# Even weight rows of the second mixer, loaded in two halves of the contraction

## The chip, the cores and the metric

The kernel runs on one core of one Trainium2 chip. The metric is the device time of one execution in microseconds (us), as a median of several runs. A profile is one further execution, recorded instruction by instruction.

## The reference

The input `x` has 2048 tokens of width 1024. A linear-attention block and a mixer over tokens follow each other, each behind a layer norm and with a residual. All inputs are bfloat16.

```python
h  = x + A(layernorm(x), wqkv, wo)      # linear attention, 32 heads
h2 = h + B(layernorm(h), w1, b1, w2, b2)

def B(x, w1, b1, w2, b2):               # S = 2048 tokens, F = 3584
    h = layernorm(x)
    u = gelu(einsum("bsd,sf->bdf", h, w1) + b1)
    y = einsum("bdf,fs->bds", u, w2) + b2
    return transpose(y)
```

The change lies in the last product, `u @ w2`: a contraction over F = 3584, with 2048 output tokens. In the text this is the second mixer; `u @ w1`'s counterpart before it is the first.

## The kernel before

**Seven products.** Each large product is made by a Strassen-like scheme of seven products instead of eight. For one pair index `p` (256 output tokens) the weights form four blocks: rows of `w2` are taken in tiles of 128, even tiles and odd tiles of the contraction, and each has two column halves of 128. The blocks `a11` and `a21` come from the even rows (`even[p % 2]`), `a12` and `a22` from the odd rows (`odd[p]`). One set of even or odd rows is a tile of 128 partitions x 14 x 256 bfloat16, 896 KB, read from HBM in runs of 512 bytes. Sums and differences of blocks (`asum`) are made by DVE. The difference for product 7 is written over `a21`, so the even rows are in use until product 7 has read them.

**Quads.** The second mixer has eight values of `p`, taken in pairs: quad `u` holds `p = 2u` and `2u + 1`. Quad 0 is the prologue, quads 1 to 3 run through `Quad.run2`. In a quad, products 1, 5, 2 and 3 of its two matrices are themselves made by a second level of seven smaller products (`Inner`, with steps `i1` to `i7`). Products 6, 7 and 4 are not; their matmuls are cut into pieces and put between the steps of the inner levels as filling (`interleave`). The last half of a quad's product 4 fills the next quad's first inner level.

**Two buffers of even rows.** There are two buffers of even rows, so the even rows of the next quad go where those of this quad lie. They can be loaded only when product 7 of the matrix in question is done. In quads 1 to 3, product 7 runs in four parts of seven matmuls each (`pieces`): the first half of the contraction for both matrices, then the second half for both. In the prologue product 7 runs whole, for one matrix and then the other.

**Order on the queues.** Most operations of this part are pinned to the order in which the program states them. All its loads go through the queue of SP (`hd`), which works in order: an issue that waits holds up those behind it. Around the change, SP has: the reload of a parked operand for product 4 (`load("p7")`, `reload(4, 0)`), which waits until both matrices' first half of product 7 has read the buffer `gs0`; the even rows of the next quad (`next2`, `load_w2(p, 0, hd)`); then, at the end of `run2`, the reload of the parked operand for product 7 (`load("in3")`), and in the next quad the odd rows (`load("in1")`). Outputs are added to HBM by accumulating stores from POOL's queue (line 487).

**Who reads the new even rows.** `begin_next` (called between the steps `i7` and `i4` of the quad's last inner level, at "third") makes the next quad's first two inner sums on DVE: the first reads the second matrix' `a11`, the next one adds the first matrix' `a11`. Step `i1` of the next quad's first inner level reads the first matrix' `a11` directly, step `i6` reads the two sums.

Line 230 is that of a helper (`Held`) that pins an operation, so most rows of this part carry L230; tiles tell them apart. `wq` is a weight tile that holds even rows, odd rows and two output buffers; `w2o` are odd rows of two further buffers; `gs` the derived moving operands for products 7 and 4; `is` the inner sums; `psI` the inner products' accumulators; `psC` that of products 7 and 4.

Of the kernel before, what the change touches and what calls it, by code (L numbers as in the profile page):

```python
# [10 lines left out]
P = 128  # L11
# [19 lines left out]
def kernel(  # L31
# [12 lines left out]
    nc = tc.nc  # L44
# [85 lines left out]
    NFP, NSP = NF // 2, NS // 2  # L130
# [20 lines left out]
    even, odd, ots = {}, {}, []  # L151
# [2 lines left out]
    def w2_view(t):  # L154
        return t.rearrange("p (k f) -> p k f", f=2 * P)

    def load_w2(p, second, q=nc.sync):
        q.dma_start(
            (odd[p] if second else even[p % 2]),
            B_w2[:, p * 2 * P:(p + 1) * 2 * P].rearrange("(k two p) s -> p k two s", two=2, p=P)[:, :, second, :],  # L160
        )

    def first_w2(p):
        t = w_tile(wpool, WLEN)
        ots.extend(t[:, 2 * WH + o:2 * WH + o + CW] for o in (0, CW))
        even[p], odd[p] = w2_view(t[:, 0:WH]), w2_view(t[:, WH:2 * WH])
        odd[p + 4] = odd[p]
        for second in (0, 1):
            load_w2(p, second)
# [63 lines left out]
    hv, ht, hs, hd = (Held(e, True) for e in (nc.vector, nc.tensor, nc.scalar, nc.sync))  # L233
# [1462 lines left out]
    spans = (slice(0, H2), slice(H2, NFP))  # L1696
# [46 lines left out]
    for p in (2, 3):  # L1743
        odd[p] = odd[p + 4] = w2b.tile([P, NFP, 2 * P], BF16, tag=f"o{p}", name=f"w2o{p}")[:]
        load_w2(p, 1)
# [5 lines left out]
    def quad2(u):  # L1751
        return Quad([Mixer2(2 * u), Mixer2(2 * u + 1)], mov1, mov5, mov2, mov3)
# [5 lines left out]
    def next2(u):  # L1758
        if u == NSP // 2:
            return None  # L1760
        for p in (2 * u, 2 * u + 1):
            load_w2(p, 0, hd)
        return quad2(u)

    def loads(u):
# [35 lines left out]
    for st in pend:  # L1801
        st.p7()
    nxt = next2(1)
    run_all(make_t4)
    pend[1].p2()
# [11 lines left out]
    for u in range(1, NSP // 2):  # L1817
        rest, nxt = nxt.run2(
            rest, lambda: next2(u + 1), loads(u), first if u == 1 else (nop,) * 4, CW - P if 2 * u + 2 == NSP else None,
        )  # L1820
# [34 lines left out]
```

## Time and profile before

| what | value |
|---|---|
| median of 3 runs | 557.47 us (557.39 to 557.54) |
| the profiled execution's own time | 559.21 us |
| its span, first to last instruction | 557.4 us |
| mean granted TensorE clock | 0.997 |
| TensorE matmul busy | 549.4 us, 99% of the span |
| DVE, ACT, POOL busy | 444.8, 289.1, 26.3 us |
| loads of even and odd rows into `wq` | 12 of 896 KB, 7.9 us to landing in the median |
| DMA over the whole span | 74.58 MB, 134 GB/s |

The page names the engines PE (TensorE matmul), PEld (its weight loads), DVE (VectorE), ACT (ScalarE), POOL (GpSimd) and SP (SyncE, which here only issues DMAs). A row of the timeline gives start, length, engine, line, operation and the tiles out<-in; in brackets stands how long the engine had been idle before it, and what released it. A row of the table of stages gives for a stretch of time the busy time of each engine, then the granted clock of TensorE, the busy share of the 16 DMA engines and their GB/s.

The second mixer begins at about 390 us; its quads 1, 2 and 3 begin at 425, 468 and 511 us.

### The profile page before, as it was taken

Reading aid. Unit: us, or ns where it says so; the run is one execution under the profiler, and the core shown is the slowest. Engines: PE = TensorE matmul, PEld = TensorE weight load, DVE = VectorE, ACT = ScalarE, POOL = GpSimd, SP = SyncE. Lnnn points to the kernel's source line nnn. Section 1 sums busy time; section 2 is a strip of 40 time slices with the busy share of each in tenths; the row PEclk is TensorE's granted clock in tenths of the full one; section 3 lists DMA queues with packets and bytes.
Section 4 is the critical chain, followed back from the end, with each engine's and each line's share of the span. In section 5 each row is a group of like instructions: output and inputs, shape, how many; then the busy total and the mean of one; then the engine's idle time right before and its main releaser. Section 6 shows DMA issues by size and latency. Waiting matters only on the chain.

```text
span 557.4 us, 9806 instructions
## 1 busy us (share of the span) xinstructions
PE 549.4 (99%) x3819; PEld 315.6 (57%) x3819; DVE 444.8 (80%) x863; ACT 289.1 (52%) x614; POOL 26.3 (5%) x36
## 2 busy tenths in 40 slices
PE   8999999999999999999999999999999998999997
PEld 3444446644444444456666666766445665667665
DVE  7798888755597798879988989788986878649747
ACT  5747778766877777635556546464112312413311
POOL 1000000000000000000000000000002102103111
PEclk9999999999999999999999999999999999999999
DMA  8933341205668932104043140440957948749433
GB/s 295 310 77 76 86 87 20 39 1 176 202 183 257 304 148 76 56 1 153 0 152 100 53 152 11 141 113 22 284 187 179 258 133 205 175 132 235 93 108 74
DMA packets 82991, 74.58 MB, mean 134 GB/s; under 512 B 15730, under 2 KB 74368, under 8 KB 82944
## 3 DMA queue, kind: packets, MB, share of 16 engines
q1 hardware_dynamic: 78560, 69.87, 42.1%
q0 software_dynamic: 4096, 3.68, 4.8%
q8 instruction: 30, 0.49, 0.4%
q10 hardware_dynamic: 288, 0.39, 0.2%
q14 instruction: 17, 0.14, 0.1%
HBM read 59.12 MB, written 11.67 MB: 127 GB/s over the span
## 4 chain that ended last, share of the span: by engine, by line
PE 94%; DMA 4%; SPq 1%; DVE 0%; ACT 0%; issue 0%; DVEq 0%
PE psI L230 24%; PE acc_t L230 15%; PE psC L230 15%; PE psB L230 8%; PE psC L973 4%; PE psB L973 4%; PE psA L973 4%; PE acc_t L893 3%; PE acc_t L1302 2%; PE psA L342 2%; PE psB L342 2%; DMA wq<-in_B_w_dram 2%; PE psE L973 2%; PE psC L342 2%; DMA wkv<-in_A_wqkv_dram 1%; PE psA L230 1%
## 5 line engine op out<-in xcount | busy, mean ns | idle before, releaser
L230 PEld LDWEIGHTS <-is 128*128 128x128 f16 x736 | 71.8, 98 | 33.7 <-DVE is L230 2.5
L230 PEld LDWEIGHTS <-sa 128*128 128x128 f16 x606 | 59.2, 98 | 27.2
L230 PEld LDWEIGHTS <-wq 128*128 128x128 bf16 (+1 forms) x496 | 48.8, 98 | 28.6 <-issue 1.0
L230 PE MATMUL acc_t<-wo_sb,pqT 128*128 128x512 f16 x256 | 55.6, 379 | 0.0
L487 POOL DMA_DIRECT2D out_dram<-wq x28 | 24.4, 935 | 519.1 <-DVE sa L334 396.3
L230 PEld LDWEIGHTS <-pqT 128*128 128x128 bf16 x256 | 24.9, 98 | 30.5 <-issue 0.6
L230 DVE TENSOR_TENSOR t<-psI,t 128x256 f32<-128x256 f32 (+1 forms) x45 | 20.8, 476 | 22.2 <-PE psI L230 20.9
L230 PE MATMUL psC<-gs,wq 128*128 128x512 f16 x140 | 34.1, 380 | 0.0
L973 PEld LDWEIGHTS <-xs 128*128 128x128 f16 x208 | 19.7, 98 | 22.3 <-DVE xs L962 0.8
L190 DVE TENSOR_SCALAR e_sb<-e_sb 128x512 bf16<-128x512 bf16 x64 | 18.4, 288 | 17.1 <-ACT e_sb L185 16.8
L230 PE MATMUL psC<-hT,sa 128*128 128x512 f16 x112 | 31.2, 380 | 0.0
L230 PE MATMUL psI<-hi,is 128*128 128x256 f16 x200 | 30.0, 273 | 0.0
L230 PE MATMUL psB<-hT,sa 128*128 128x512 f16 x112 | 29.7, 380 | 0.0
L230 PE MATMUL acc_t<-xnT,wq_sb 128*128 128x512 bf16 x128 | 29.0, 380 | 0.0
L230 DVE BATCH_NORM_STATS2 hst<-acc_t 128x6 f32<-128x512 f32 x32 | 21.4, 692 | 8.9 <-ACT h_bf L230 8.9
L185 ACT ACTIVATE e_sb<-acc_t 128x512 bf16<-128x512 f32 x32 | 19.1, 597 | 17.3 <-PE acc_t L1302 9.5
L973 PE MATMUL psA<-wkv,xnT 128*128 128x512 bf16 x104 | 26.7, 379 | 0.0
L973 PEld LDWEIGHTS <-xnT 128*128 128x128 bf16 x156 | 15.2, 98 | 18.7 <-issue 1.1
L230 DVE TENSOR_TENSOR e<-psI,es 128x256 f32<-128x256 f32 x20 | 8.5, 425 | 20.8 <-PE psI L230 20.8
L230 ACT CAST h_bf<-acc_t 128x512 bf16<-128x512 f32 x32 | 18.4, 584 | 12.4 <-PE acc_t L230 12.0
L230 PE MATMUL psI<-gi,is 128*128 128x256 f16 x168 | 22.7, 276 | 2.0 <-DVE is L230 2.0
L230 PE MATMUL psC<-hT,wq 128*128 128x512 f16 x96 | 24.6, 379 | 0.0
(245 smaller groups left out, 1117.3 us busy)
## 6 DMA issues: line engine op xcount, KB each, us to landing
wq<-in_B_w_dram SPq DMA_DIRECT2D x14, 1024.0 KB, 7.8
wq<-in_B_w_dram SPq DMA_DIRECT2D x12, 896.0 KB, 7.9
gs<-parked SPq DMA_DIRECT2D x9, 896.0 KB, 4.9
shared_sb<-rd_dram SPq DMA_DIRECT2D x32, 128.0 KB, 4.2
out_dram<-h_bf SPq DMA_DIRECT2D x16, 256.0 KB, 2.0
x_sb<-in_A_x_dram SPq DMA_DIRECT2D x14, 256.0 KB, 3.0
w2o<-in_B_w_dram SPq DMA_DIRECT2D x4, 896.0 KB, 10.2
out_dram<-wq POOLq DMA_DIRECT2D x28, 128.0 KB, 5.1
```

The source lines that it names most:

```text
L185: pin(nc.scalar.activation(e_sb[:], src, ACT.Exp))
L190: pin(nc.vector.tensor_scalar(e_sb[:], e_sb[:], 1.0, PHI_EPS, ALU.min, ALU.add))
L230: return (lambda *a, **kw: pin(op(*a, **kw))) if self.always or getattr(Held, self.key) else op
L342: pe.matmul(ps[:, cols], lhsT=lhs[:, k, :], rhs=mv(k)[:, cols], start=(start and k == 0), stop=(k == self.nk - 1), skip_group_check=True,)
L487: nc.gpsimd.dma_start(to, ot[:, a:b], accum_op=ALU.add)
L893: mm = nc.tensor.matmul(pp[:, 0:CW], lhsT=xnT[:, kt, i * P:(i + 1) * P], rhs=wkv[:, kt, c * CW:(c + 1) * CW], start=(kt == 0), stop=(kt == ...
L973: pin(nc.tensor.matmul(ps[:], lhsT=lhs[:, k, :], rhs=rhs[:, k, :], start=(start and k == 0), stop=(k == hk2 - 1), skip_group_check=True,))
L1302: nc.tensor.matmul(qp[:, 0:SW], lhsT=wq_sb[:, kt, j * P:(j + 1) * P], rhs=xnT[:, kt, u * SW:(u + 1) * SW], start=(kt == 0), stop=(kt == ND ...
```

## The change

`load_w2` gets a range of the contraction, `ks`, which is all 14 tiles unless given. `next2` loads the even rows of the next quad's two matrices in two halves of 7 tiles: first the first half of both matrices, then the second half of both. A load of 896 KB becomes two of 448 KB; runs remain 512 bytes. As the first halves overwrite only the first seven tiles of each buffer, they have to wait only for the first half of product 7. Nothing else is moved. `spans` is `(slice(0, 7), slice(7, 14))`, which was there before.

```diff
-    def load_w2(p, second, q=nc.sync):
+    def load_w2(p, second, q=nc.sync, ks=slice(0, NFP)):
         q.dma_start(
-            (odd[p] if second else even[p % 2]),
-            B_w2[:, p * 2 * P:(p + 1) * 2 * P].rearrange("(k two p) s -> p k two s", two=2, p=P)[:, :, second, :],
+            (odd[p] if second else even[p % 2])[:, ks, :],
+            B_w2[:, p * 2 * P:(p + 1) * 2 * P].rearrange("(k two p) s -> p k two s", two=2, p=P)[:, ks, second, :],
         )
...
     def next2(u):
         if u == NSP // 2:
             return None
-        for p in (2 * u, 2 * u + 1):
-            load_w2(p, 0, hd)
+        for ks in spans:
+            for p in (2 * u, 2 * u + 1):
+                load_w2(p, 0, hd, ks)
         return quad2(u)
```

`next2` is called three times, for quads 1, 2 and 3.

## The prediction

> **What bounds the kernel now.** First the page: one engine fills the span, so only an idle or slow stretch of TensorE can be worth anything.
>
> ```profile
> PE 549.4 (99%) x3819; PEld 315.6 (57%) x3819; DVE 444.8 (80%) x863; ACT 289.1 (52%) x614; POOL 26.3 (5%) x36
> ```
>
> The list of waits for 400 to 557 us, where the second mixer runs, then says where TensorE stops and what stands behind it. Columns: who waited for whom, total us, times, longest.
>
> ```profile
> DVE is L255 <- DMA wq<-in_B_w_dram: 4.2, 1, 4.2
> ...
> DVE is L230 <- DMA wq<-in_B_w_dram: 2.5, 1, 2.5
> ...
> PE psI L230 <- DVE is L230: 2.0, 1, 2.0
> ```
>
> DVE waits twice for the even rows that the change touches. Only one of these waits reaches TensorE, once, for 2.0 us. The timeline shows that place, the start of quad 2 (first column: start in us; second: length; in brackets: idle before and its releaser).
>
> ```profile
> 453.53 0.34 SPq L230 DMA_DIRECT2D gs<-parked  x1
> ...
> 456.57 2.64 SPq L230 DMA_DIRECT2D wq<-in_B_w_dram  x2
> ...
> 467.79 0.93 PE L230 MATMUL psI<-gE,wq 128*128 128x256 f16 x7
> ...
> 470.25 0.63 DVE L230 TENSOR_TENSOR is<-wq 128x896 f16<-128x896 bf16 x1 [2.54 <-DMA wq<-in_B_w_dram]
> ...
> 471.60 1.38 PE L230 MATMUL psI<-gi,is 128*128 128x256 f16 x7 [2.02 <-DVE is L230]
> ...
> 475.67 0.93 PE L230 MATMUL psI<-gE,is 128*128 128x256 f16 x7
> ```
>
> The table of stages, cut to 1 us, adds the clock (the column after POOL is PEclk, then the DMA share and GB/s).
>
> ```profile
> 457.00:458.00 1.00, 1.00 (x7) 0.51 (x6) 0.66 (x2) 0.20 (x1) 0.00 (x0) 1.00 0.46 146
> 458.00:459.00 1.00, 1.00 (x8) 0.60 (x7) 0.97 (x2) 0.52 (x1) 0.18 (x1) 1.00 0.99 268
> ...
> 470.00:471.00 1.00, 0.00 (x0) 0.00 (x0) 0.71 (x2) 0.00 (x0) 0.00 (x0) 1.00 1.02 316
> ...
> 473.00:474.00 1.00, 1.00 (x6) 0.72 (x5) 1.00 (x2) 0.36 (x1) 0.83 (x1) 0.50 0.00 0
> ```
>
> The idle is followed by half clock. The clock record puts it at 471.94 to 475.35, the only such stretch between 4.3 us and the end.
>
> **The price of that stall.** From the start of i1 (467.79) to the start of i5 (475.67) quad 2 takes 7.88 us. The same instructions of quad 3 run from 511.18 to 515.20, 4.02 us, without idle and at full clock. So the stall costs 3.86 us. TensorE's work before i6 would have let it start at 469.41 and it started at 471.60, which is 2.19; the other 1.67 are the slow clock.
>
> **Why the load is late.** A DMA adds one to its completion count for each of the 16 DMA engines. Quad 2 holds the matrices p4 and p5 (pair indices 4 and 5). The counts say that the load for p4 (issued 456.57) was done on 15 engines at 462.00 and on the last at 464.55. The load for p5 (issued 458.84) was done at 466.94 and 470.23. One DMA engine was 3.29 us behind. The sums take 1.37 us from landing to i6 (470.23 to 471.60), so the last landing that costs nothing is 469.41 - 1.37 = 468.04; it came 2.19 too late. In quad 3 the loads had landed by 510.02 and DVE reached its sums only at 511.02; that quad gains nothing. In quad 1 DVE waits 4.17 us and has its sums at 424.93, i6 starts at 427.94, with no idle before it: it gains nothing either and stands 3.0 us of lateness.
>
> **The change, part by part.**
>
> Removed and moved: two loads of 896 KB become four of 448 KB, three times. In quads 2 and 3 the queue of SP is in order: the reload for product 4 (t4, 453.53) stays ahead, because it waits for the first half of the seventh products of both matrices, and that is also what both first halves wait for. They follow at once, at about 453.9 and 454.3 (one issue takes 0.37). The second halves wait for what the whole loads waited for: 456.57 and 458.84. So half of the bytes are issued 2.7 and 4.5 us earlier.
>
> How much earlier does the last byte land? The DMA engines had no work left only for a while: share 0.46 in 457 to 458 and 0.99 or about that from there on. So 0.54 us of transfer can move ahead; with the ramp of 455 to 456 (share 0.75) 0.79. Rows of 512 bytes went at 482 per us before the stores came (2894 packets from 458 to 464), which is 33 ns each on an engine, so 16 to 24 packets of each engine move. At the end they stand in turn with the accumulating stores of 1024 bytes (101 ns a packet, from 463.9). By the packets that were left, 15 engines end near 465.5 instead of 466.94. If the last engine keeps its lag it ends near 469.2, 1.0 earlier; if its lag is 2.5 us or less, as it was for p4, it ends by 468.05 and the stall is gone. So the idle left lies between 0 and 1.2 us; I take 0.5. An idle of 0.54 us at 6.2 us in this trace was not followed by a slow clock, and 2.02 was; so I count no slow clock. Gain in the profiled execution: 3.86 - 0.5 = 3.36. Ends: 0.8 (0.8 us less idle, the slow clock stays) and 3.86.
>
> The Trainium skill, "TensorE: Matmul & The Clock Gate", Part 1, says that the clock halves after at least one idle window of about 3.4 us. By it 2.0 us of idle would cost no slow clock, and the whole stall 2.19 instead of 3.86; this trace shows 3.41 us of half clock behind 2.02 of idle, so the measurement decides.
>
> Added: two more issues on SP per quad, 0.37 us each. What SP has next in quad 2 is the reload at 467.21, 8 us after; nothing is late. The fixed part of two more transfers: at the first mixer two loads were issued 0.44 us apart (255.99, 256.43) and landed 5.2 and 8.0 us after issue, so a queued load takes 3.2 us more and not another 5.2. The fixed part lies beside the load ahead, and I count nothing; not covered, it would be 5.2 - 3.2 = 2.0 us, which would use up the advance.
>
> The page "DMA: Bandwidth & Descriptors", section "Measured (HBM→SBUF, 128 partitions, SWDGE, issued from GpSimd)", speaks against the change: it wants transfers of 1 MiB or more, and its fit of 2.0 us and the bytes makes a load of 448 KB 3.1 us, so four in a row 12.2 where two of 896 KB take 8.2, an estimate of 4 us lost. No run here shows halves of this load alone.
>
> More waits: DVE's first sum reads p5 whole, the second p4, TensorE's i1 p4; each now waits for two transfers. The first of each pair has landed by then, so nothing is added; the bound from the trace is one gap of an issue, 0.02 us in the chain of waits, to six times that.
>
> In quad 1 the seventh products of the two matrices run one behind the other (410.29 to 416.34). SP would issue the first halves for matrices 2 and 3 at about 411.8 and 414.9, then the second half for 2 at 415.2 instead of 413.35, that for 3 at 416.4 as now. The last landing stays within about 1 us of 423.63, under the 3.0 to spare. What is next late: with the stall gone nothing, by quad 3.
>
> **From the trace to the time.** The profiled execution took 559.21 us, of which the span is 557.44 and 1.77 lie around it. The median of the runs is 557.47, 1.74 below. The trace doesn't say what these 1.74 are; they may be a shorter stall. So the gain in a timed run lies between 3.36 - 1.74 = 1.62 and 3.36, middle 2.5: 557.47 - 2.5 = 555.0. Its own range runs from the full 3.86 (553.6) to the least that can be told, 1.1 (556.4): the measurement tells about 0.2%, 1.1 us, from no change.
>
> **The rivals.**
>
> Same, 0.33: the late DMA engine belongs to this one execution. No other load behind 190 us has a lag over 1.2 us between the 15th and 16th engine. With a lag of 1.1 us p5's load would land at 468.04, exactly in time; then timed runs have no stall to lose, and the time stays at 557.2 to 557.6. Against it: the three runs agree within 0.15 us, and 1.74 is less than 3.86. The same result comes if the halves are not kept apart and the first ones wait for the whole seventh products: landing as before, 557.5. Against that: at 413.35 a part of tile wq is loaded while TensorE still has to read its other part (416.17).
>
> Slower, 0.17: the reload of the operand of product 4 (t4) no longer has the DMA engines to itself. It landed at 458.38 and its first reader ran at 460.18, 1.80 to spare (501.86 and 503.57 in quad 3, 1.71). Alone it takes 4.9 us; rows of the same transfer with a load 0.4 us behind it show 5.0 (479.45) and 6.0 (436.06), both inside that. Beyond 1.8 us it decides: with the lag of 3.29 on it, it lands at 457.90 + 3.29 = 461.19, TensorE stops for 1.0 and may lose 1.67 in clock. Where the old stall doesn't exist in timed runs, that is 557.47 + 1.0 to 2.7, 558.5 to 560.2.
>
> **How the numbers follow.** Faster 0.50 at 555.0 (553.6 to 556.4), same 0.33, slower 0.17. From 553.5 to 558.4 leaves out nearly all of the slower case, and a little below.
>
> **What would show it.** Right: four issues per quad, two right behind the reload near 454; the load's last landing before 468.04; no 2 us gap before i6, no half clock at 472; i1 to i5 of quad 2 near 4.0 us. Wrong: the first halves issued near 456.6; an equal landing; a gap before the first psC behind the reload of t4; or a stall-free quad 2 with an unchanged time, which would put the stall down to the one execution.

## The result, and the profile after

| | kernel before | changed kernel |
|---|---|---|
| median of 6 runs, us | 557.43 (557.12 to 557.72) | 555.52 (555.29 to 556.6) |
| ratio to the kernel before | | 0.9968, interval 0.9956 to 0.9981 |
| profiled execution's own time, us | 559.21 | 556.6 |
| its span, us | 557.4 | 554.8 |

By the medians the changed kernel is faster by 1.91 us, 0.34%. The ratios here and below are not those of the medians; they differ from them by up to 0.0013. The forecast was 555.0, in a range of 553.5 to 558.4.

The chain of waits on the page of the changed kernel has no DMA left in it (before, 4% of it was):

```profile
PE 98%; issue 0%; ACT 0%; DVE 0%; DVEq 0%
```

The list of waits for 400 to 557 us keeps one of the three rows shown before, that of quad 1. DVE still waits there, a little longer, and TensorE does not:

```profile
DVE is L255 <- DMA wq<-in_B_w_dram: 4.5, 1, 4.5
```

The timeline at quad 2 (start, length, engine; everything before it lies 1.18 us later than in the trace of before; the shift arises in the first 13 us, where this execution's clock came up at 10.6 us and not at 4.3):

```profile
454.71 0.34 SPq L230 DMA_DIRECT2D gs<-parked  x1
...
455.15 5.25 SPq L230 DMA_DIRECT2D wq<-in_B_w_dram  x4
...
468.81 0.62 DVE L230 TENSOR_TENSOR is<-wq 128x896 f16<-128x896 bf16 x1
...
468.97 0.93 PE L230 MATMUL psI<-gE,wq 128*128 128x256 f16 x7
...
470.60 0.93 PE L230 MATMUL psI<-gi,is 128*128 128x256 f16 x7
...
472.99 0.93 PE L230 MATMUL psI<-gE,is 128*128 128x256 f16 x7
```

Four issues begin right behind the reload. DVE's first sum and i6 have lost their bracketed waits. From i1 to i5 it is 472.99 - 468.97 = 4.02 us instead of 7.88, which is what quad 3 took. Laid over each other by instruction, the two traces stand 1.18 us apart from 13 us on to i6 of quad 2 and -2.68 behind i5; so the change's whole effect in the trace, 3.86 us, arises at this one place.

The table of stages in 1 us, at the two places that carried the argument (after POOL: clock, DMA share, GB/s):

```profile
457.00:458.00 1.00, 1.00 (x9) 0.60 (x8) 0.14 (x1) 0.00 (x0) 0.00 (x0) 1.00 1.03 423
458.00:459.00 1.00, 1.00 (x9) 0.61 (x7) 0.47 (x2) 0.02 (x1) 0.00 (x0) 1.00 0.94 333
...
470.00:471.00 1.00, 1.00 (x8) 0.61 (x7) 1.00 (x4) 0.79 (x2) 0.81 (x1) 1.00 0.74 287
```

The slack of 457 to 458 (share 0.46) is gone: the reload runs straight into the first halves. TensorE is busy through 470 to 471 at full clock.

### The profile page after: what moved, and what is told of

The parts are those of the page before. It is cut to its first block, busy times and chain, and to the rows that moved or that the text cites. A ratio compares the mean times of both kernels' runs of the same rounds, so it can differ in the third digit from the quotient of the medians.

```text
span 554.8 us, 9799 instructions
## 1 busy us (share of the span) xinstructions
PE 548.8 (99%) x3801; PEld 316.3 (57%) x3819; DVE 444.6 (80%) x863; ACT 289.0 (52%) x614; POOL 26.3 (5%) x36
## 4 chain that ended last, share of the span: by engine, by line
PE 98%; issue 0%; ACT 0%; DVE 0%; DVEq 0%
PE psI L230 25%; PE psC L230 16%; PE acc_t L230 15%; PE psB L230 8%; PE psC L973 4%; PE psB L973 4%; PE psA L973 4%; PE acc_t L893 4%; PE acc_t L1302 2%; PE psB L342 2%; PE psA L342 2%; PE psE L973 2%; PE psC L342 2%; PE psA L230 1%; PE psE L342 1%; PE acc_t L97 1%
## 5 line engine op out<-in xcount | busy, mean ns | idle before, releaser
L230 ACT COPY psI<-psI 128x256 f32<-128x256 f32 x50 | 18.0, 360 | 11.6 <-PE psI L230 9.7
```

Source lines behind the costliest of these rows:

```text
L230: return (lambda *a, **kw: pin(op(*a, **kw))) if self.always or getattr(Held, self.key) else op
```

## A measure for the experiments

The experiments are compared in one number, read from the completion counts of the trace: the time from the issue of the reload for product 4 (453.53 in the trace of before) to the last landing of the next quad's even rows, on 15 of the 16 DMA engines and on the last; the lag is the difference of the two. In the trace of before the landing that costs nothing is at 468.04, 14.51 us behind that issue; in quad 3 it is as far (i6 at 512.80, less 1.37, less 496.92). "Gap" is TensorE's idle time before i6 of quad 2 (e8: within i1, after four of its seven matmuls, and before i6).

| kernel, its profiled execution | 15 engines | last | lag | gap |
|---|---|---|---|---|
| before | 13.41 | 16.70 | 3.29 | 2.02 |
| changed | 11.21 | 13.70 | 2.50 | none |
| e1, before again | 13.44 | 13.48 | 0.04 | none |
| e2, halves in quad 2 only | 11.39 | 12.11 | 0.72 | none |
| e2, its quad 3 | 13.25 | 15.85 | 2.60 | 1.16 |
| e3, halves in quads 1 and 3 | 13.46 | 13.48 | 0.01 | none |
| e4, second half first | 13.46 | 15.39 | 1.93 | 0.78 |
| e5, before, fetch moved | 13.31 | 13.38 | 0.07 | none |
| e6, before, four stores out | 11.97 | 14.29 | 2.32 | none |
| e7, changed, 448 KB more | 15.68 | 15.73 | 0.05 | 1.12 |
| e8, changed, 896 KB more | 17.06 | 17.65 | 0.58 | 1.01 + 1.85 |
| e9, changed again | 11.00 | 13.51 | 2.51 | none |
| e10, quad 2 only again | 11.43 | 13.29 | 1.86 | none |
| e10, its quad 3 | 13.37 | 14.81 | 1.44 | 0.13 |
| e11, changed, fetch moved | 10.92 | 10.93 | 0.01 | none |

Every row over 14.51 has a gap, and no row under it has one. The column for 15 engines hardly moves from one execution of a kernel to the next (13.25 to 13.46 in the rows where nothing is issued earlier and the stores run); the lag of the last engine does, from 0 to 3.3 us.

## The experiments

The runs of e1 to e4, of e5 to e8 and of e9 to e11 were taken on one chip each, beside runs of the kernel before: medians of 557.46 (35 runs), 557.05 (29) and 557.33 (26). "Low" counts runs under 556.1 us, a line drawn afterwards. A run above it need not have a stall: the profiled execution of the changed kernel took 556.6 us with no gap, by its slow start.

| kernel | median, us | ratio to before, interval | low |
|---|---|---|---|
| before, all three chips | | | 21 of 90 |
| e1 before again | 557.56 | 1.0005, 0.9992 to 1.0019 | 2 of 12 |
| e2 halves in quad 2 only | 555.08 | 0.9965, 0.9953 to 0.9977 | 10 of 12 |
| e3 halves in quads 1 and 3 | 556.33 | 0.9979, 0.9963 to 0.9996 | 6 of 12 |
| e4 second half first | 556.93 | 0.9999, 0.9987 to 1.0011 | 1 of 12 |
| e5 before, fetch moved | 555.33 | 0.9980, 0.9966 to 0.9995 | 10 of 12 |
| e6 before, four stores out | 555.89 | 0.9988, 0.9975 to 1.0001 | 9 of 12 |
| e7 changed, 448 KB more | 557.33 | 1.0015, 0.9999 to 1.0030 | 0 of 12 |
| e8 changed, 896 KB more | 559.29 | 1.0053, 1.0033 to 1.0073 | 0 of 6 |
| e9 changed again | 555.45 | 0.9967, 0.9954 to 0.9980 | 10 of 12 |
| e10 quad 2 only again | 555.22 | 0.9967, 0.9951 to 0.9984 | 10 of 12 |
| e11 changed, fetch moved | 555.33 | 0.9960, 0.9945 to 0.9975 | 9 of 9 |

**e1, the kernel before again** (no edit).

> The kernel before, once more, as its own comparison. The theory (a regular stall at the start of quad 2, made by one late DMA engine): a gap on TensorE before i6 of quad 2 again, with half clock behind it, i1 to i5 near 7.9 us in the profile, a lag of 2.5 to 3.3 us on the 16th DMA engine at the second load, and about 557.4 us. The rival (the late engine belonged to one execution): no gap, i1 to i5 near 4.0 us, a lag of 1.2 us or less. The timed runs lay 1.74 us under the profiled one; if their mean granted clock is 1.000 where the profiled run has 0.997, their stall has no slow clock.

Measured: 557.56 us, but the profiled execution was one of the two low ones, 555.82 us, with a lag of 0.04 and no gap. So neither side was right as stated. The stall is not of one execution: 10 of these 12 runs, and 69 of 90 of the others, lie above 556.1, mostly near 557.4. It is not in every execution either: the profile shows none. The other timed runs have no trace, so what separates them is inferred: the median of the 21 low ones of the 90 is 555.3 and that of the others 557.5, which makes the typical stall 2.2 us. As for the slow clock, a mean clock of 0.997 or less stands with 4 of these 102 runs, one of them at 557.16; the others above the line have 0.999 or 1.000. Of the 90, 17 lie at 558.0 to 559.4, 14 of them at 0.999 or more; what lengthens those stays open.

**e2, halves in quad 2 only.**

```diff
-        for ks in spans:
+        for ks in spans if u == 2 else (slice(0, NFP),):
```

> Halves for quad 2 alone, whole loads for quads 1 and 3. The theory: all of the gain, 555.5 us (1.9 below the kernel before), i1 to i5 of quad 2 at 4.02 us. The rival (the gain is made by the split as such, at all three places, or by another order in the prologue): about a third of it, 556.8 us.

Measured: 555.08 us, all of the gain. The profiled execution was one of the two that are higher (556.9), and shows why: quad 2 is clean, and the whole load for quad 3 has a lag of 2.60. In its timeline, quad 3:

```profile
508.92 0.62 DVE L230 TENSOR_TENSOR is<-wq 128x896 f16<-128x896 bf16 x1 [1.70 <-DMA wq<-in_B_w_dram]
...
510.26 0.94 PE L230 MATMUL psI<-gi,is 128*128 128x256 f16 x7 [1.16 <-DVE is L230]
```

The stall of quad 2 is the one that matters most, and quad 3 has the same weak place.

**e3, halves in quads 1 and 3 only.**

```diff
-        for ks in spans:
+        for ks in (slice(0, NFP),) if u == 2 else spans:
```

> Halves for quads 1 and 3, a whole load for quad 2. The theory: no gain, 557.4 us, the gap before i6 of quad 2 as in the kernel before. The rival (gain at all three places): two thirds of it, 556.1 us.

Measured: 556.33 us, with no run at that value: six lie at 554.8 to 555.5 and six at 557.1 to 558.5. Theory and rival both miss. Read by its two groups it fits a stall that comes or not; that it came in half of the runs and not in three quarters as in the kernel before may in part be quad 3, which e2 shows to stall at times. Twelve runs don't settle it, and the one profile lies in the low group.

**e4, four halves without the earlier issue.**

```diff
-        for ks in spans:
-            for p in (2 * u, 2 * u + 1):
+        for p in (2 * u, 2 * u + 1):
+            for ks in reversed(spans):
                 load_w2(p, 0, hd, ks)
```

> Four loads of half the size, but for each matrix the second half first, so that nothing can be issued before the whole seventh product has read the rows. The theory (what counts is the earlier issue): the landing in quad 2 stays where it was within 0.5 us, the gap stays, 557.4 us (557.0 to 558.0). The rival (smaller transfers or their order are what helps): about 555.5 us, without the gap. A second rival (a cost of 2 us for each further transfer): 559 us or more, with a landing 2 to 4 us later.

Measured: 0.9999 of before, and 15 engines done at 13.46, where the kernel before has 13.41 and 13.44. So halves as such bring nothing, and two further transfers cost nothing that can be told, not 2 us each. The waits of its profile from 400 to 557 us:

```profile
DVE is L230 <- DMA wq<-in_B_w_dram: 1.3, 1, 1.3
...
PE psI L230 <- DVE is L230: 0.8, 1, 0.8
```

**e5, the instruction fetch moved.** One of the DMA queues brings instructions; its row on the page, alike in both kernels (packets, MB, share of 16 engines):

```profile
q8 instruction: 30, 0.49, 0.4%
```

Thirty packets of 16 KB for some 7600 rows of TensorE: one for each 255 of its instructions in the mean, by one DMA engine in 0.9 to 1.5 us. In the trace of before one runs at 457.27, while the reload ends and just before the first rows of quad 2's load (457.61).

```diff
-            mm(warm[:, 0:P], warm[:, 0:BANK])
+            for c in range(0, BANK, P):
+                mm(warm[:, 0:P], warm[:, c:c + P])
```

> The kernel before, with the ten warm-up matmuls at the start cut into four of 128 columns each, which adds 60 instructions to TensorE's stream. Each 16 KB instruction fetch holds 256 of these, so the fetch that falls into the load of quad 2 (457 us) should come some 4 us earlier, before the load begins, and leave the DMA engine on which it runs free of it. Theory 1 (the fetch starts the lag of the 16th DMA engine): lag under 1 us, no gap before i6 of quad 2 in most runs, 555.4 us. Theory 2 (the lag comes by itself): about 557.4 us as before. If it lies between, the fetch has a share.

Measured: 555.33 us, 10 of 12 runs low, where 9 of the 29 runs of before were on the same chip. The fetch came at 451.94, 1.7 us ahead of the reload instead of 3.7 behind it, and the lag was 0.07. The kernel before, with no change to any load, gains 1.7 us by the medians (1.1 by the ratio, 0.3 to 1.9), which can't be told from what the change gains. This speaks for theory 1. On the first of the two whole loads of quad 2 the lag was 2.55, 0.88, 0.80 and 3.02 us with the fetch in its place (before, e1, e3, e6) and 0.07 here, so in quad 2 the fetch most likely starts the lag. But the edit moves every later fetch as well; no run moves this one alone. It is not the only source of a lag: the whole load of quad 3 in e2 had 2.60 with the last fetch ended 3 us before that load's first issue, and in e1 and e3 the fetch fell at the same place and the lag was made up by the second load. Why the lag grows from the 1 us of a fetch to 2.5 or 3.3 in one execution and vanishes in another stays open.

**e6, four stores left out.** The stores that follow the load onto the DMA engines (matrices 2 and 3, two of four blocks each) are not issued.

```diff
-                nc.gpsimd.dma_start(to, ot[:, a:b], accum_op=ALU.add)
+                if self.p not in (2, 3) or (sh, dh) not in ((0, 0), (1, 1)):
+                    nc.gpsimd.dma_start(to, ot[:, a:b], accum_op=ALU.add)
```

> The kernel before, with four of its accumulating stores left out (matrices 2 and 3, the ones issued at 458.8 to 462.3 us); those parts of the output are missing. Theory 1 (the rows still to come at 464 us are slowed by standing in turn with the stores): the load's last landing comes 1.5 to 3 us earlier, without any change in its issue, no gap in quad 2, 555.3 us. Theory 2 (the stores don't matter, the DMA engine is late for another reason): landing and gap as before, 557.4 us.

Measured: in the profile 15 engines are done at 11.97, 1.3 to 1.5 us earlier than with whole loads of quad 2 and the stores (13.31 to 13.46), and with a lag of 2.32 the last landing still comes before 14.51; no gap. So the stores hold up the 15 engines, and the late one lags without them too. The time, 555.89, does not separate from before by its interval, though all its runs lie below 18 of the 29 of before. It is also 0.5 us above e5; its profile has 3.99 us behind the last matmul of the program where e5's has 3.50, which I can't explain.

**e7 and e8, the landing pushed back.** Ahead of the first halves of quad 2, one more transfer from HBM to HBM (1792 columns in e7, 3584 in e8).

```diff
+        if u == 2:
+            hd.dma_start(dram.tile([P, 1792], BF16, name="extra")[:], B_w1[0:P, 0:1792])
         for ks in spans:
```

> The changed kernel, with a further transfer of 448 KB between two places in HBM issued ahead of the first halves of quad 2, so that the load lands later. The theory (DMA engines are full there, so each transfer ahead of the load moves its landing by its own length): 448 KB at 0.25 to 0.28 MB per us make 1.6 to 1.8 us; in the profile of the changed kernel 0.8 us were to spare, so 0.8 to 1.0 us of idle, no slow clock, 1 us slower than the changed kernel, 556.5 us. The rival (there is more to spare, the landing isn't what counted): 555.5 us as without it.

> As the one before, with 896 KB. The theory: 3.3 to 3.6 us later, 2.5 to 2.8 us of idle before i6 of quad 2, 558.0 to 558.3 us without a slow clock, up to 1.7 more in runs that get one (a mean clock of 0.997). The rival: 555.5 us.

Measured: 557.33 and 559.29 us, 1.8 and 3.8 above the 555.52 of the changed kernel, more than expected by 0.8 and 1.0 to 1.3. The idle was a little more than expected (1.12 and 2.86), its price was not as expected: i6 starts 0.2 to 0.3 us later than the idle shows, and 8 us behind a gap there is a second one of 0.18 us, which adds 0.4 us of delay. Laid by instruction over e1's profile, which has no gap, i6 is late by 1.28 in e7 and 3.20 in e8, and TensorE behind the second gap by 1.69 and 3.62, near the 1.8 and 3.8 of the medians (e2's quad 3: 1.16 of idle, i6 late by 1.33, 1.74 with the second gap). That a transfer ahead moves the landing by its own length holds roughly for the last engine, 2.0 and 4.0 later than in the changed kernel's profile. On 15 engines it was 4.5 and 5.9: some 1500 of the load's 3584 rows were still to come when the stores began, against 183 in the changed kernel. The waits in the profile of e7:

```profile
DVE is L230 <- DMA wq<-in_B_w_dram: 1.6, 1, 1.6
...
PE psI L230 <- DVE is L230: 1.1, 1, 1.1
```

and of e8, where the load is late enough to hold i1 too, which reads the rows directly (four of its seven matmuls run, the other three wait):

```profile
PE psI L230 <- DVE is L230: 1.9, 1, 1.9
...
PE psI L230 <- DMA wq<-in_B_w_dram: 1.0, 1, 1.0
```

So the landing is what counts, and the changed kernel has little to spare, 0.8 us in its profile: 448 KB use it up. A mean clock of 0.997 or less stands with one of 12 runs of e7 and two of 6 of e8, but not with the profile of e8, where 1.01 and 1.85 us of idle stand with 1.4 us of work between them.

**e9, e10, e11, three versions on one chip.** e9 is the changed kernel, e10 is e2, e11 is the changed kernel with the edit of e5.

> The changed kernel once more, as the mark for the next two. 555.1 to 555.6 us with no gap in quads 2 and 3 in nearly all runs; if one run in six or more lies 1.5 us higher, the change only lowers the odds of the stall.

> Halves for quad 2 alone, on the same chip as the changed kernel. Theory 1 (only quad 2 stands in a fetch, and the 0.4 us between 555.08 and 555.52 were another chip's): the same as the changed kernel within 0.2 us, with a few more runs that have a gap in quad 3. Theory 2 (the halves cost something where they bring nothing): 0.4 us faster than the changed kernel.

> The changed kernel with the warm-up matmuls cut into four, so that the fetch misses the load of quad 2. The theory (both edits remove the same stall): nothing on top, the same as the changed kernel within 0.2 us. The rival (they remove different things): 1.5 to 2 us below it, 553.5 us.

Measured: 555.45, 555.22 and 555.33 us. All three lie within 0.25 us and can't be told apart; none beats the changed kernel beyond doubt. e10 has two runs at 556.8 and its profiled execution a gap of 0.13 in quad 3. In e9 the lag was there again (2.51), and the landing still came in time. In e11 it was 0.01; the two remedies bring nothing on top of each other, so they remove the same stall. Whether the two runs of e9 at 556.4 and 556.6 had a stall can't be said without a trace.

## Why the prediction was right, and where it was off

**The mechanism held.** The halves were issued at 455.15 and 455.62, 0.44 and 0.91 behind the reload (predicted: at about 0.4 and 0.8), the DMA engines were filled where they had run empty, quad 1 went as forecast (last landing 0.2 us later than before, less the shift, and no idle), the landing of quad 2 came before the point that costs nothing, and the stall of 3.86 us of the profiled execution went. e2 shows that it is quad 2, e4 that it is the earlier issue, e7 and e8 that it is the landing.

**The landing moved by more than the sum had it.** Predicted for 15 engines was 1.4 us (466.94 to 465.5); measured is 2.0 to 2.5 (13.41 to between 10.92 and 11.43 from the reload). For the last engine with its lag kept, 1.0 was predicted; it is 3.0, of which 0.8 is that the lag was 2.50 and not 3.29. The term that was mis-sized is the 16 to 24 rows that each engine gets ahead. At 9.8 us behind the reload's issue the profiles with whole loads of quad 2 (before, e1, e5) have 702 to 804 of the 3584 rows still to come, those with earlier halves (changed, e2, e9, e10, e11) 160 to 269: 27 to 40 rows for each engine. I had taken the DMA engines to be full from 458 on, because their share stood near 1. It was no ceiling: the table of stages of the changed kernel has 1.12 and 1.22 in 459 to 461, and with the halves queued 558 to 581 rows went per us between 4.5 and 9.8 us behind the reload, against 503 to 523. So when the stores began (464.51), 183 rows were left in the changed kernel, where before there were 611 (463.93). The late engine still had some 20 of its rows to go when the others were done, and took 0.12 us for each of them, in turn with the stores; it came in time because all ended earlier. So the 0.5 us of idle that I left in were none.

**The slow clock was priced wrongly for the timed runs.** I took the profiled execution's stall, 1.67 us of slow clock included, and an unknown 1.74 between it and the median, and went half way. The runs make it likely what the 1.74 were: the profiled execution of before had a slow clock, as 4 of 102 further runs had; the typical stall has none and costs some 2.2 us. Without the slow clock the sum is 3.86 - 1.67 = 2.19 against a measured 1.91; it lies within the interval (1.1 to 2.5 us), and no run shows what makes the rest. That the forecast came within 0.5 us of the time is in part luck: 2.5 was the middle between a gain that priced the profiled stall too low (3.36 for 3.86) and one that took an unexplained 1.74 off it.

**The rule of the clock.** The Trainium skill, "TensorE: Matmul & The Clock Gate", Part 1, wants one idle window of 3.4 us for the slow clock. The gaps of 0.78, 1.12, 1.16 and 1.01 + 1.85 us in the profiles of e4, e7, e2 and e8 were followed by none, in its favour; the one of 2.02 in the profile of before was followed by 3.41 us of it, against.

**The rule of large transfers.** "DMA: Bandwidth & Descriptors", section "Measured (HBM→SBUF, 128 partitions, SWDGE, issued from GpSimd)", with the fit of its section "Anatomy of one DMA — SWDGE (gpsimd) path", would have had four halves 4 us later, by the estimate in the prediction. Both sections are on transfers issued from GpSimd; these loads are issued from SP. e4 measures it: 13.46 instead of 13.41 to 13.44 on 15 engines. Here, behind other loads, the fixed part doesn't show; the row of the two loads at 256 us was the better guide.

**The rivals.** "The late engine belongs to this one execution" is refuted as stated and has a true part: the lag differs from profile to profile, and about one timed run of before in four is as short as one without the stall. "Slower, by the reload" did not come: with halves behind it the reload took 4.47 us in the changed kernel, against 4.85 before. What I said of quad 3, that it gains nothing, holds for the profiled execution only: e2 and e10 show gaps there with a whole load.

## What to carry to other kernels

When a wait is seen in a single profile, ask how far the landing on 15 of the 16 DMA engines lies from the point that costs nothing: here 1.1 us of slack, which the lag of one engine (0 to 3.3 us) used up in some executions and not in others (three timed runs of four are as long as a stall makes them), and 3.1 to 3.6 us with the earlier issue, which it did not in any of five profiles. A DMA share near 1 is no proof that no more could be moved: here it reached 1.2. Splitting this load paid only through the part that could be issued earlier; the split itself neither helped nor cost (e4). Price a stall for timed runs without the slow clock that one profile shows behind it, unless several executions show it.

## What was not expected

- A 16 KB instruction fetch for TensorE, one for each 255 of its instructions, takes one DMA engine 0.9 to 1.5 us. Where it falls very likely has a share in whether a stall comes: 60 further instructions at the start of the program moved one by some 5 us and gained the kernel before about as much as the change does (0.9980, interval 0.9966 to 0.9995).
- The four accumulating stores of 128 KB behind the load pushed its landing back by 1.3 to 1.5 us on 15 engines (e6), although they were issued after the first of its two transfers.
- A gap on TensorE (0.13 to 1.85 us) was followed by a second one of 0.18 us 8 us later, in all five profiles that had one in quad 2 or 3 without a slow clock.
